# Reordering the head of a Strassen GEGLU kernel: the first product of chunk 1 and its additions earlier, the first products in halves, the last block copied whole

## The chip, the cores and the metric

The kernel runs on one core of one Trainium2 chip. Its engines are called PE (TensorE), DVE (VectorE), ACT (ScalarE), POOL (GpSimd) and SP (SyncE, which here only issues DMAs). PSUM is the memory, in banks, into which PE writes its products. The metric is the device time in microseconds (us); lower is better. Each profile is of one execution, and "the page" is the profiler's summary of it; its times count from that execution's first instruction, and "the span" is from the first to the last instruction, about 1.8 us less than the reported time.

## The reference

```python
def reference(x, w_gate, w_up, w_down):
    return (_gelu(x @ w_gate) * (x @ w_up)) @ w_down
# x: 32 x 32 x 1024 (1024 tokens of 1024), w_gate and w_up: 1024 x 3584, w_down: 3584 x 1024, all bf16
# _gelu is the tanh approximation
```

## The kernel before

Both matrix products are done by one level of the Strassen-Winograd scheme, seven products of quarter matrices instead of eight. The hidden columns of the first product go in chunks of two 128-column tiles. Chunk 0 is computed plainly, without Strassen, because its products can begin while most of x is still on its way. From chunk 1 on, TensorE (PE) multiplies sums: S1 to S4 are sums of weight quarters, T1 to T4 sums of quarters of x (b11, b12, b21, b22, transposed by the DMA but for the first part of b21). P1 is `b11` times the first quarter of the gate weights. For ten column tiles the product of `b21` with the second quarter is kept ahead: it is made in the head, copied out of PSUM to `ahead`, and added to P1 later by VectorE (DVE).

One rule of this layout matters here. P1 stays in its PSUM bank and S2*T2 is accumulated onto it. So DVE must have read P1 (the addition `c`, `c = ahead + psA`) **before** PE may start S2*T2.

The parts that the change and the argument touch (cuts marked with `...`):

```python
BANKS = {"A": 4, "B": 2, "C": 2}          # PSUM banks by tag, 128 x 512 f32 each
...
# the first quarter-tiles of b21 are transposed on PE, half by DVE, half by ACT:
for dt in range(KQ):
    for half in range(2):
        ...                                # two transposes into tp
        (nc.vector.tensor_copy, nc.scalar.copy)[half](b21[:, dt, half * hw : (half + 1) * hw], tp)
nc.tensor.matmul(warm_ps[:, : NB // 2], ...)     # a filler of 256 columns
...
for k in range(KQ):                        # the first real products
    for j in range(KB):
        product_ahead(ps[j], 0, j, k, k + 1)
...
tt(t1, b12, b11, SUB)                      # T1 on DVE
for fl in range(FC):                       # chunk 0, first 512 tokens
    ...
    plain_out(fl, 0, *tok0[fl])            # GELU on ACT, times up on DVE: "lo<-h,ps"
tok1 = [(acc("A"), acc("C")) for _ in range(FC)]
...
tt(t2, b22, t1, SUB)                       # T2
nc.scalar.copy(b22r, b22)
chunk1 = sums(1, nc.vector)
for _ in range(3):
    next(chunk1)                           # S1, S2, S4 of chunk 1 on DVE
for fl in range(FC):                       # chunk 0, second 512 tokens
    ...
    plain_out(fl, 1, *tok1[fl])
...
for j, tag in enumerate("BB"):             # the last two products kept ahead
    ps = acc(tag)
    product_ahead(ps, 2, j)
    nc.scalar.copy(ahead[2][:, j, :], ps)
...
tt(t3, b22, b12, SUB)                      # T3
begun = [first_product(FC + fl) for fl in range(FC)]   # P1, then c = ahead + P1, then GELU
next(chunk1)                               # S3
tt(t4, b21, t2, SUB)                       # T4
nc.gpsimd.tensor_copy(ident[:, :1], t4[:, 0, :1])      # POOL may start its sums only after T4
...
# in every chunk: S1*T1 in banks C, then S2*T2 onto P1 in banks A, then S4*b22 in C,
# then P1 of the next chunk, S3*T3 in A
...
# the last output block, copied in two halves by two engines from one bank:
for copy, queue, c0 in ((nc.vector.tensor_copy, nc.sync, 0), (nc.scalar.copy, nc.scalar, NB // 2)):
    o = late.tile([P, NB // 2], bf16, name="o_end", tag="o_end", bufs=2)
    copy(o, banka[m][:, c0 : c0 + NB // 2])
    queue.dma_start(out=of[r0 : r0 + P, c0 : c0 + NB // 2], in_=o)
```

Of the kernel before, what the change touches and what calls it, by code (L numbers as in the profile page):

```python
# [13 lines left out]
def kernel(  # L14
# [20 lines left out]
    nc = tc.nc  # L35
    P = nc.NUM_PARTITIONS
    fp32 = mybir.dt.float32
    f32r = mybir.dt.float32r
    bf16 = mybir.dt.bfloat16
    tt = nc.vector.tensor_tensor  # L40
    ADD, SUB, MUL = ALU.add, ALU.subtract, ALU.mult

    xf = x.flatten_outer_dims()
    of = out.flatten_outer_dims()
    N, D = xf.shape
    F = w_gate.shape[1]
    NB = 512
    assert N == 2 * NB and D == 2 * NB and F % (4 * P) == 0
    DT, FT = D // P, F // P
    KD = DT // 2  # L50
    FC = 2
# [4 lines left out]
    MT = NB // P  # L56
    NWARM = 6
    KB = 4
# [32 lines left out]
    def by_batch(tiles):  # L91
        def at(k):
            b = next(i for i, (k0, k1) in enumerate(batches) if k < k1)
            return tiles[b][:, k - batches[b][0], :]

        return at

    def g_of(ft):
        k = ft % HF
        return by_batch(g_lo if ft < HF else g_hi)(k)  # L100
# [3 lines left out]
    def acc(tag):  # L104
        return ps1.tile([P, NB], fp32, name=f"ps{tag}", tag=tag, bufs=BANKS[tag])
# [4 lines left out]
    b11 = xpool.tile([P, KD, NB], bf16, name="b11")  # L110
    b21 = xpool.tile([P, KD, NB], bf16, name="b21")
    b12 = ring.tile([P, KD, NB], bf16, name="b12", tag="ring")
    b22 = ring.tile([P, KD, NB], bf16, name="b22", tag="ring")
    t1, t2, t3, t4, b22r = (xpool.tile([P, KD, NB], f32r, name=n) for n in ("t1", "t2", "t3", "t4", "b22r"))

    def x_rows(dt, nb):
# [3 lines left out]
    ahead = [  # L120
        gpool.tile([P, n, NB], fp32, name="ahead", tag=f"hi{n}", bufs=2) for n in (KB, KB, QF - KB)
    ]
# [13 lines left out]
    def load_w_all(ci, which):  # L136

        alloc_w(ci, which)
        load_w(nc.sync, ci, which, 0, KD if which == 0 and is_ahead(ci) else DT)

    def is_ahead(ci):
        return 0 < ci and (ci + 1) * FC <= FC + NAHEAD

    def quads(ci, fl=None):
        cols = slice(None) if fl is None else slice(fl * P, (fl + 1) * P)
        wg, wu = w_tiles[ci, 0], w_tiles[ci, 1]
        a12 = wg[:, KD:, cols]
        if is_ahead(ci):
            i, j = divmod((ci - 1) * FC, KB)
            a12 = a12_ahead[i][:, :, j * P : (j + FC) * P][:, :, cols]  # L150
        return wg[:, :KD, cols], a12, wu[:, :KD, cols], wu[:, KD:, cols]
# [23 lines left out]
    ones_w = nc.const_aps.tensor(1.0, [P, P], bf16)  # L175
    ones_m = nc.const_aps.tensor(1.0, [P, NB], bf16)
# [6 lines left out]
    with tc.manual_schedule():  # L183
        for eng, p0, p1 in ((nc.sync, 0, HALF), (nc.scalar, HALF, NB_P)):
            eng.dma_start(
                out=x_nat[:, p0:p1, :],
                in_=xf[p0 * P : p1 * P, KD * P : (KD + KQ) * P].rearrange("(b p) d -> p b d", p=P),
# [34 lines left out]
        warm_ps = acc("A")  # L222
# [3 lines left out]
        for dt in range(KQ):  # L226
            for half in range(2):
                hw = HALF * P
                tag = next(tags)
# [3 lines left out]
                        tp[:, b * P : (b + 1) * P], x_nat[:, half * HALF + b, dt * P : (dt + 1) * P], ident  # L233
                    )
                (nc.vector.tensor_copy, nc.scalar.copy)[half](b21[:, dt, half * hw : (half + 1) * hw], tp)
        nc.tensor.matmul(warm_ps[:, : NB // 2], lhsT=ones_w, rhs=ones_m[:, : NB // 2], start=True, stop=True)

        def plain(ps, which, fl, nb, d0, d1, first=0, last=DT - 1):
            for dt in range(d0, d1):
                nc.tensor.matmul(  # L240
                    ps,
                    lhsT=w_tiles[0, which][:, dt, fl * P : (fl + 1) * P],
                    rhs=x_rows(dt, nb),
                    start=(dt == first),
                    stop=(dt == last),
                )

        def gelu(src, tag, bufs):
            h = ework.tile([P, NB], bf16, name=tag, tag=tag, bufs=bufs)
            nc.scalar.activation(h, src, ACT.Gelu_apprx_tanh)  # L250
            return h

        def plain_out(ft, nb, gate, up):
            tt(g_of(ft)[:, nb * NB : (nb + 1) * NB], gelu(gate, "h0", 4), up, MUL)  # L254

        def prod(ps, lhs, rhs, start):
            for k in range(KD):
                nc.tensor.matmul(  # L258
                    ps,
                    lhsT=lhs[:, k, :],  # L260
                    rhs=rhs[:, k, :],
                    start=(start and k == 0),
                    stop=(k == KD - 1),
                    skip_group_check=True,
                )

        def ahead_of(ft):
            i, j = divmod(ft - FC, KB)
            return ahead[i][:, j, :]

        def product_ahead(ps, i, j, k0=0, k1=KD):
            for k in range(k0, k1):
                nc.tensor.matmul(
                    ps,
                    lhsT=a12_ahead[i][:, k, j * P : (j + 1) * P],
                    rhs=b21[:, k, :],
                    start=(k == 0),
                    stop=(k == KD - 1),
                )


        ps = [acc(t) for t in "CCAA"]
        tok0 = [(acc("A"), acc("B")) for _ in range(FC)]

        def plain0(d0, d1):
            for which in (0, 1):
                for dt in range(d0, d1):
                    for fl in range(FC):
                        plain(tok0[fl][which], which, fl, 0, dt, dt + 1, KD, KD - 1)

        for k in range(KQ):
            for j in range(KB):
                product_ahead(ps[j], 0, j, k, k + 1)
        plain0(KD, KD + KQ)
        for j, copy in enumerate((nc.scalar.copy, nc.vector.tensor_copy) * 2):
            product_ahead(ps[j], 0, j, KQ)
# [7 lines left out]
        for j, tag in enumerate("CCAA"):  # L304
            ps = acc(tag)
            product_ahead(ps, 1, j)
            (nc.scalar.copy, nc.vector.tensor_copy)[j % 2](ahead[1][:, j, :], ps)
        tt(t1, b12, b11, SUB)
        for fl in range(FC):
            for which in (0, 1):  # L310
                plain(tok0[fl][which], which, fl, 0, 0, KD, KD, KD - 1)
            plain_out(fl, 0, *tok0[fl])
        tok1 = [(acc("A"), acc("C")) for _ in range(FC)]
        for fl in range(FC):
            for which in (0, 1):
                plain(tok1[fl][which], which, fl, 1, 0, KD)
# [5 lines left out]
        for fl in range(FC):  # L322
            for which in (0, 1):
                plain(tok1[fl][which], which, fl, 1, KD, DT)
            plain_out(fl, 1, *tok1[fl])
        load_w_all(2, 1)
        for j, tag in enumerate("BB"):
            ps = acc(tag)
            product_ahead(ps, 2, j)
            nc.scalar.copy(ahead[2][:, j, :], ps)  # L330


        def added(s, ps):
            t = ework.tile([P, NB], fp32, name="c", tag="c", bufs=3)
            tt(t, s, ps, ADD)  # L335
            return t

        def snap(ps, tag):
            t = ework.tile([P, NB], fp32, name=tag, tag=tag, bufs=2)
            nc.scalar.copy(t, ps)  # L340
            return t

        def first_product(ft):
            psa = acc("A")
            prod(psa, quads(*divmod(ft, FC))[0], b11, True)
            if ft < FC + NAHEAD:
                return psa, gelu(added(ahead_of(ft), psa), "h0", 4)
            return psa, snap(psa, "sn1")

        def last_product(st):  # L350
            ft, psa, h0 = st
            prod(psa, a22rs.pop(ft), t4, False)
            tt(g_of(ft)[:, :NB], h0, psa, MUL)  # L353

        tt(t3, b22, b12, SUB)  # L355
        begun = [first_product(FC + fl) for fl in range(FC)]
        next(chunk1)
        tt(t4, b21, t2, SUB)

        nc.gpsimd.tensor_copy(ident[:, :1], t4[:, 0, :1])  # L360
        open_fts = []
        for ci in range(1, NCH):
            fts = range(ci * FC, (ci + 1) * FC)
# [8 lines left out]
            sn5, sn2, h1, h0 = [], [], [], []  # L372
            psa, first = zip(*begun)
# [16 lines left out]
            if fts[0] < FC + NAHEAD:  # L390
                h0 = first
            else:
                for fl in range(FC):
                    psb = acc("B")
                    prod(psb, quads(ci, fl)[1], b21, True)
                    h0.append(gelu(added(first[fl], psb), "h0", 4))
            begun = [first_product(ft + FC) for ft in fts] if ci + 1 < NCH else []
            for fl, ft in enumerate(fts):
                prod(psa[fl], s3[fl], t3, False)
# [51 lines left out]
        late = ctx.enter_context(tc.tile_pool(name="late", bufs=1))  # L451
# [35 lines left out]
        banka = [acc("A") for _ in range(MT)]  # L487
# [69 lines left out]
        product(banka, by_batch(a22r), by_batch(tch), tail=QF)  # L557
        for m in range(MT):
            r0 = NB + m * P
            if m < MT - 1:  # L560
                o = late.tile([P, NB], bf16, name="o_sb", tag="o_sb", bufs=MT)
                (nc.vector.tensor_copy if m % 2 == 0 else nc.scalar.copy)(o, banka[m])
                nc.scalar.dma_start(out=of[r0 : r0 + P, :NB], in_=o)
                continue

            for copy, queue, c0 in ((nc.vector.tensor_copy, nc.sync, 0), (nc.scalar.copy, nc.scalar, NB // 2)):
                o = late.tile([P, NB // 2], bf16, name="o_end", tag="o_end", bufs=2)
                copy(o, banka[m][:, c0 : c0 + NB // 2])
                queue.dma_start(out=of[r0 : r0 + P, c0 : c0 + NB // 2], in_=o)
# [1 line left out]
_INS = ['x', 'w_gate', 'w_up', 'w_down']  # L571
_OUTS = [((32, 32, 1024), 'bfloat16')]
# [25 lines left out]
```

## Time and profile before

| kernel before | value | where it is read |
|---|---|---|
| time, first three runs | 275.81 us median (275.01 to 275.81) | the timed runs |
| span of the profiled run | 273.6 us | the page |
| PE busy | 269.1 us, 98% | the page's first part |
| PE's end | 269.98 us | the timeline |
| hole in the first Strassen chunk | about 0.4 us | matmul starts in the trace |
| PE's end to the last landing of output data | 2.51 us | the trace |

From the page of the kernel before, the span, PE's busy time and the chain of waits by engine:

```profile
span 273.6 us, 3349 instructions
...
PE 269.1 (98%) x1199; PEld 187.9 (69%) x1199; DVE 198.1 (72%) x195; ACT 111.4 (41%) x183; POOL 108.1 (40%) x55
...
PE 87%; SPq 5%; DVE 4%; DMA 2%; issue 1%; ACT 0%; DVEq 0%
```

PE is the limit, so only time in which PE stands still can be won. The chain, followed back from the end, is PE for 87% of the span, but its start runs over the DMA queue (SPq), a DMA and DVE. That is the place the change works on.

PE's timeline of before where the plain products end and chunk 1 begins (start, duration, engine, source line, operation, out<-in, size, count; groups overlap because the end of a matmul is modelled). In order: the two products kept ahead, P1, S1*T1, S2*T2, S4*b22, P1 of chunk 2.

```profile
25.30 1.89 PE L273 MATMUL psB<-b,a12b 128*128 128x512 bf16 x8
27.03 1.89 PE L258 MATMUL psA<-b,wg 128*128 128x512 bf16 x8
28.57 2.21 PE L258 MATMUL psC<-t,s 128*128 128x512 f32 x8
30.84 2.11 PE L258 MATMUL psA<-t,s 128*128 128x512 f32 x8
32.80 1.99 PE L258 MATMUL psC<-b22r,s 128*128 128x512 f32 x8
34.63 1.90 PE L258 MATMUL psA<-b,wg 128*128 128x512 bf16 x8
```

From S1*T1 to S2*T2 pass 2.28 us, where 2.02 to 2.03 is the pace elsewhere. PE's weight loads (PEld) name the cause, in brackets: the idle time just before, and what ended it.

```profile
30.84 1.68 PEld L258 LDWEIGHTS psA<-t,s 128*128 128x128 f32 x8 [0.50 <-DVE c L335]
```

DVE's timeline of before shows what stood ahead of that addition. In order: T1, two GELU products, T2, S1, S2, S4, two GELU products, T3, and then `c`.

```profile
17.45 2.29 DVE L308 TENSOR_TENSOR t<-b,b 128x2048 fp32r<-128x2048 bf16 x1 [1.62 <-DMA b<-in_x_dram]
19.66 1.28 DVE L254 TENSOR_TENSOR lo<-h,psB 128x512 bf16<-128x512 bf16 x2
20.86 2.29 DVE L317 TENSOR_TENSOR t<-b,t 128x2048 fp32r<-128x2048 bf16 x1
23.06 1.22 DVE L162 TENSOR_TENSOR s<-wu 128x1024 fp32r<-128x1024 bf16 x1
24.31 1.22 DVE L163 TENSOR_TENSOR s<-s,wg 128x1024 fp32r<-128x1024 f32 x1
25.57 1.22 DVE L164 TENSOR_TENSOR s<-a12a,s 128x1024 fp32r<-128x1024 bf16 x1
26.71 1.28 DVE L254 TENSOR_TENSOR lo<-h,psC 128x512 bf16<-128x512 bf16 x2
27.91 2.29 DVE L355 TENSOR_TENSOR t<-b,b 128x2048 fp32r<-128x2048 bf16 x1
30.11 1.28 DVE L335 TENSOR_TENSOR c<-ahead,psA 128x512 f32<-128x512 f32 x2
```

DVE works without a pause from 17.45 to the addition.

Last, the tail of before, after PE's end at 269.98 (CAST is the copy out of PSUM, DMA_DIRECT2D the issue of a store on the queue of SyncE or ACT):

```profile
270.02 0.42 DVE L568 CAST o_end<-psA 128x256 bf16<-128x256 f32 x1 [0.90 <-PE psA L421]
270.47 0.36 SPq L569 DMA_DIRECT2D out_dram<-o_end  x1
270.48 0.37 ACT L568 CAST o_end<-psA 128x256 bf16<-128x256 f32 x1 [3.04 <-DVE o_end L568]
270.88 0.34 ACTq L569 DMA_DIRECT2D out_dram<-o_end  x1
```

The two half copies run one after the other; ACT waited for DVE.

### The profile page before, as it was taken

The numbers are of one execution on the slowest core, as the hardware profiler recorded it, in microseconds if no ns is written. First come the engines' busy times: TensorE is split into PE (matmuls) and PEld (weight loads), VectorE is DVE, ScalarE is ACT, GpSimd is POOL, SyncE is SP. The second block draws the span as 40 slices with busy tenths as digits, with TensorE's granted clock in tenths as the row PEclk, the third lists the DMA queues.
The fourth block names the chain that finished last, engine by engine and source line by source line (L and its number), as shares of the span: only waits on it lengthen the run. The fifth ranks groups of instructions, "written<-read, shape, count | busy, mean of one in ns | idle before, by whom it ended". The sixth has DMA issues, their size and how long they took to land.

```text
span 273.6 us, 3349 instructions
## 1 busy us (share of the span) xinstructions
PE 269.1 (98%) x1199; PEld 187.9 (69%) x1199; DVE 198.1 (72%) x195; ACT 111.4 (41%) x183; POOL 108.1 (40%) x55
## 2 busy tenths in 40 slices
PE   8999999999999999999999999999999999999994
PEld 3444677877878677676868676764447888888883
DVE  0269997987966676666657656459999999999511
ACT  2263565454643646555463636430300023962001
POOL 1000089999897695948577574000000000000000
PEclk9999999999999999999999999999999999999999
DMA  7994330414504505050514280004992445695202
GB/s 173 282 240 127 101 90 25 117 42 114 156 16 137 146 8 157 0 153 1 154 35 120 74 274 0 0 2 163 350 293 79 134 134 189 216 285 194 78 0 78
DMA packets 53393, 33.77 MB, mean 123 GB/s; under 512 B 8704, under 2 KB 53376, under 8 KB 53376
## 3 DMA queue, kind: packets, MB, share of 16 engines
q1 hardware_dynamic: 50384, 31.13, 39.4%
q10 hardware_dynamic: 2992, 2.43, 2.7%
q8 instruction: 9, 0.15, 0.2%
q14 instruction: 8, 0.07, 0.1%
HBM read 29.62 MB, written 2.10 MB: 116 GB/s over the span
## 4 chain that ended last, share of the span: by engine, by line
PE 87%; SPq 5%; DVE 4%; DMA 2%; issue 1%; ACT 0%; DVEq 0%
PE psA L258 34%; PE psA L421 18%; PE psC L258 17%; PE psC L421 7%; PE psB L421 7%; PE psB L258 5%; SPq L205 3%; DMA b<-in_x_dram 2%; DVE lo L254 1%; SPq L134 1%; DVE t L355 1%; DVE t L317 1%; SPq L194 1%; DVE s L163 0%; DVE s L162 0%
## 5 line engine op out<-in xcount | busy, mean ns | idle before, releaser
L258 PE MATMUL psA<-t,s 128*128 128x512 f32 x208 | 54.3, 403 | 0.1
L250 ACT ACTIVATE h<-c 128x512 bf16<-128x512 f32 x52 | 31.8, 630 | 38.9 <-DVE c L335 38.9
L258 PEld LDWEIGHTS psA<-t,s 128*128 128x128 f32 x208 | 39.0, 188 | 9.7 <-DVE c L335 0.5
L162 POOL TENSOR_TENSOR s<-wu 128x1024 fp32r<-128x1024 bf16 x12 | 26.8, 2232 | 23.4 <-DMA wu<-in_w_up_dram 14.0
L335 DVE TENSOR_TENSOR c<-sn,psA 128x512 f32<-128x512 f32 x26 | 17.8, 683 | 16.8 <-PE psA L258 16.5
L258 PEld LDWEIGHTS <-wg 128*128 128x128 bf16 x168 | 15.4, 98 | 20.1 <-issue 3.4
L163 POOL TENSOR_TENSOR s<-s,wg 128x1024 fp32r<-128x1024 f32 x12 | 27.8, 2314 | 0.9
L165 POOL TENSOR_TENSOR s<-wg,wu 128x1024 fp32r<-128x1024 bf16 x12 | 27.1, 2255 | 0.0
L340 ACT COPY sn<-psC 128x512 f32<-128x512 f32 x26 | 15.2, 588 | 27.1 <-PE psC L258 23.0
L340 ACT COPY sn<-psA 128x512 f32<-128x512 f32 x42 | 23.4, 585 | 6.2 <-PE psA L258 6.1
L258 PE MATMUL psC<-t,s 128*128 128x512 f32 x104 | 25.9, 391 | 0.0
L258 PE MATMUL psA<-t,a22r 128*128 128x512 f32 x104 | 25.9, 391 | 0.0
L258 PE MATMUL psC<-b22r,s 128*128 128x512 f32 x104 | 25.7, 389 | 0.0
L258 PE MATMUL psA<-b,wg 128*128 128x512 bf16 x104 | 24.6, 380 | 0.0
L258 PEld LDWEIGHTS psC<-t,s 128*128 128x128 f32 x104 | 19.5, 188 | 4.2
L258 PEld LDWEIGHTS psA<-t,a22r 128*128 128x128 f32 x104 | 19.5, 188 | 4.1
L258 PEld LDWEIGHTS psC<-b22r,s 128*128 128x128 f32 x104 | 19.5, 188 | 4.1
L400 DVE TENSOR_TENSOR lo<-c,h 128x512 bf16<-128x512 f32 x12 | 21.5, 1794 | 0.6
L335 DVE TENSOR_TENSOR c<-sn,psC 128x512 f32<-128x512 f32 x26 | 17.7, 687 | 5.1 <-PE psC L258 5.1
L353 DVE TENSOR_TENSOR hi<-h,psA 128x512 bf16<-128x512 bf16 x14 | 9.6, 688 | 14.2 <-PE psA L258 14.2
L164 POOL TENSOR_TENSOR s<-wg,s 128x1024 fp32r<-128x1024 bf16 x8 | 17.3, 2159 | 0.6
L464 ACT COPY snb<-psC 128x512 f32<-128x512 f32 x4 | 2.2, 590 | 36.5 <-PE psC L421 22.7
(101 smaller groups left out, 411.9 us busy)
## 6 DMA issues: line engine op xcount, KB each, us to landing
wu<-in_w_up_dram SPq DMA_DIRECT2D x13, 512.0 KB, 4.0
wdb<-in_w_down_dram SPq DMA_DIRECT2D x12, 512.0 KB, 4.8
wdb<-in_w_down_dram SPq DMA_DIRECT2D x12, 384.0 KB, 4.1
wg<-in_w_gate_dram SPq DMA_DIRECT2D x8, 512.0 KB, 5.1
v<-in_w_down_dram SPq DMA_DIRECT2D x4, 512.0 KB, 6.4
out_dram<-o_sb ACTq DMA_DIRECT2D x15, 128.0 KB, 1.7
wg<-in_w_gate_dram SPq DMA_DIRECT2D x6, 256.0 KB, 4.5
v<-in_w_down_dram SPq DMA_DIRECT2D x4, 384.0 KB, 7.8
```

Of the source, the lines that this page charges most:

```text
L162: yield eng.tensor_tensor(s1, a21, a22, ADD)
L163: yield eng.tensor_tensor(s2, s1, a11, SUB)
L164: yield eng.tensor_tensor(s4, a12, s2, SUB)
L165: yield eng.tensor_tensor(s3, a11, a21, SUB)
L205: nc.sync.dma_start_transpose(out=t[:, d0 % KD : (d1 - 1) % KD + 1, :], in_=xf[nb * NB : (nb + 1) * NB, d0 * P : d1 * P])
L250: nc.scalar.activation(h, src, ACT.Gelu_apprx_tanh)
L258: nc.tensor.matmul(ps, lhsT=lhs[:, k, :], rhs=rhs[:, k, :], start=(start and k == 0), stop=(k == KD - 1), skip_group_check=True,)
L335: tt(t, s, ps, ADD)
L340: nc.scalar.copy(t, ps)
L353: tt(g_of(ft)[:, :NB], h0, psa, MUL)
L400: tt(g_of(ft)[:, NB:], added(sn5[fl], psa[fl]), h1[fl], MUL)
L421: nc.tensor.matmul(banks[m], lhsT=lhs(k)[:, m * P : (m + 1) * P], rhs=rhs(k), start=(start and k == 0), stop=(k == HF - 1), skip_group_che ...
```

## The change

The intent is to let no wait stand in front of PE at the head, and to shorten the tail. It has three pieces. Piece 1: P1 of chunk 1 goes ahead of the last two products kept ahead (which move from banks B to C, as the second tokens' up products move from C to B); its additions go ahead of T3, S3 and T4 and of the second tokens' GELU products; T1 follows the first GELU product. Piece 2: the filler goes, and the first four products are done in halves of 256 columns, so that the halves that DVE copies can be used before ACT has copied the others. Piece 3: the last block is copied whole.

```diff
-        nc.tensor.matmul(warm_ps[:, : NB // 2], lhsT=ones_w, rhs=ones_m[:, : NB // 2], start=True, stop=True)
...
         for k in range(KQ):
-            for j in range(KB):
-                product_ahead(ps[j], 0, j, k, k + 1)
+            for cols in (slice(0, NB // 2), slice(NB // 2, NB)) if k == 0 else (slice(None),):
+                for j in range(KB):
+                    product_ahead(ps[j], 0, j, k, k + 1, cols)
...
-        tt(t1, b12, b11, SUB)
         for fl in range(FC):
             for which in (0, 1):
                 plain(tok0[fl][which], which, fl, 0, 0, KD, KD, KD - 1)
-            plain_out(fl, 0, *tok0[fl])
-        tok1 = [(acc("A"), acc("C")) for _ in range(FC)]
+            plain_out(fl, 0, gelu(tok0[fl][0], "h0", 4), tok0[fl][1])
+            if fl == 0:
+                tt(t1, b12, b11, SUB)
+        tok1 = [(acc("A"), acc("B")) for _ in range(FC)]
...
-            plain_out(fl, 1, *tok1[fl])
+            tok1[fl] = gelu(tok1[fl][0], "h0", 4), tok1[fl][1]
         load_w_all(2, 1)
-        for j, tag in enumerate("BB"):
-            ps = acc(tag)
-            product_ahead(ps, 2, j)
-            nc.scalar.copy(ahead[2][:, j, :], ps)
...
+        p1 = [acc("A") for _ in range(FC)]
+        for fl in range(FC):
+            prod(p1[fl], quads(1, fl)[0], b11, True)
+        for j, tag in enumerate("CC"):
+            ps = acc(tag)
+            product_ahead(ps, 2, j)
+            nc.scalar.copy(ahead[2][:, j, :], ps)
+        begun = [first_product(FC + fl, p1[fl]) for fl in range(FC)]
         tt(t3, b22, b12, SUB)
-        begun = [first_product(FC + fl) for fl in range(FC)]
         next(chunk1)
         tt(t4, b21, t2, SUB)
 
         nc.gpsimd.tensor_copy(ident[:, :1], t4[:, 0, :1])
+        for fl in range(FC):
+            plain_out(fl, 1, *tok1[fl])
...
         for m in range(MT):
             r0 = NB + m * P
-            if m < MT - 1:
-                ...
-                continue
-            for copy, queue, c0 in ((nc.vector.tensor_copy, nc.sync, 0), (nc.scalar.copy, nc.scalar, NB // 2)):
-                ...
+            o = late.tile([P, NB], bf16, name="o_sb", tag="o_sb", bufs=MT)
+            (nc.vector.tensor_copy if m % 2 == 0 else nc.scalar.copy)(o, banka[m])
+            nc.scalar.dma_start(out=of[r0 : r0 + P, :NB], in_=o)
```

More of the change, by code (lines that the diff above doesn't have):

```diff
@@ L251, in gelu, with plain_out @@
             return h
-        def plain_out(ft, nb, gate, up):
-            tt(g_of(ft)[:, nb * NB : (nb + 1) * NB], gelu(gate, "h0", 4), up, MUL)
+        def plain_out(ft, nb, h, up):
+            tt(g_of(ft)[:, nb * NB : (nb + 1) * NB], h, up, MUL)
         def prod(ps, lhs, rhs, start):
@@ L269, in ahead_of, with product_ahead @@
             return ahead[i][:, j, :]
-        def product_ahead(ps, i, j, k0=0, k1=KD):
+        def product_ahead(ps, i, j, k0=0, k1=KD, cols=slice(None)):
             for k in range(k0, k1):
                 nc.tensor.matmul(
-                    ps,
+                    ps[:, cols],
                     lhsT=a12_ahead[i][:, k, j * P : (j + 1) * P],
-                    rhs=b21[:, k, :],
-                    start=(k == 0),
+                    rhs=b21[:, k, cols],
+                    start=(k == 0 and not cols.start),
                     stop=(k == KD - 1),
+                    skip_group_check=True,
                 )
@@ L341, in snap, with first_product @@
             return t
-        def first_product(ft):
-            psa = acc("A")
-            prod(psa, quads(*divmod(ft, FC))[0], b11, True)
+        def first_product(ft, psa=None):
+            if psa is None:
+                psa = acc("A")
+                prod(psa, quads(*divmod(ft, FC))[0], b11, True)
             if ft < FC + NAHEAD:
@@ L559 @@
             r0 = NB + m * P
-            if m < MT - 1:
-                o = late.tile([P, NB], bf16, name="o_sb", tag="o_sb", bufs=MT)
-                (nc.vector.tensor_copy if m % 2 == 0 else nc.scalar.copy)(o, banka[m])
-                nc.scalar.dma_start(out=of[r0 : r0 + P, :NB], in_=o)
-                continue
-            for copy, queue, c0 in ((nc.vector.tensor_copy, nc.sync, 0), (nc.scalar.copy, nc.scalar, NB // 2)):
-                o = late.tile([P, NB // 2], bf16, name="o_end", tag="o_end", bufs=2)
-                copy(o, banka[m][:, c0 : c0 + NB // 2])
-                queue.dma_start(out=of[r0 : r0 + P, c0 : c0 + NB // 2], in_=o)
+            o = late.tile([P, NB], bf16, name="o_sb", tag="o_sb", bufs=MT)
+            (nc.vector.tensor_copy if m % 2 == 0 else nc.scalar.copy)(o, banka[m])
+            nc.scalar.dma_start(out=of[r0 : r0 + P, :NB], in_=o)
 _INS = ['x', 'w_gate', 'w_up', 'w_down']
```

## The prediction

> **What bounds the kernel now.** TensorE: the page's first part has PE busy 269.1 of 273.6 us (98%), the chain of waits is 87% PE. Consecutive matmul starts in the trace (0.216 us apart in bf16, about 0.227 in f32) show only these holes after the warm-up: about 0.1 us before the first product (start 4.58), 0.42 us in the first Strassen chunk (28.57 to 34.63: 6.07 us where later chunks' pace gives 5.65), and 3.6 us after PE's end at 269.97.
>
> **Piece 1, P1's additions ahead (the core).** In the timeline S2*T2 starts at 30.84; its weight load waited 0.50 us for DVE's addition `c`, which stood in DVE's queue behind T1, T2, S1, S2, S4, four GELU products and T3 (2.29) and ran at 30.11. After: P1 runs on PE at about 25.2 to 27, the two last kept-ahead products follow, and DVE adds right after S4. S1 needs w_up, which lands at 22.83, S2 w_gate at 23.67, so I expect the additions at about 26.5 to 27.8, some 2.5 us before PE wants them. T3, S3, T4 end near 30, 31.2, 33.4, all before their products. The two delayed GELU products end near 34.6; DVE's next addition starts as before. POOL's sums, released by T4, start 1.5 us earlier. The hole closes: -0.40.
>
> T1 after the first GELU product costs DVE 0.1 us (b12 lands only at 17.35). The second tokens' up products now use the B banks; the second is freed near 20.5, wanted at 20.9: the tightest new wait, at most 0.3 us. The C banks of the kept-ahead products are copied by ACT about 0.1 us before S1*T1 wants them: possible +0.1.
>
> **Piece 2, first products in halves, filler matmul gone.** The matmul work is equal (eight of 256 columns for four of 512); the filler filled a wait. The first half can start at about 4.3, but the second needs the bank that ACT is copying until 4.53: at most 0.1 us won. That is then lost again: the next weights landed at 6.06 with PE loading them at 6.10, the a12 weights at 7.94 with the load at 7.98. I give it 0 to -0.05. The clock is full at 4.25 already (256 columns took 273 ns); the Trainium skill ("TensorE: Matmul & The Clock Gate", What's actually happening) has the throttle released after about 3.4 us of activity, which fits the warm-up from 0.77 to about 4.1 here.
>
> **Piece 3, last block whole.** Now DVE (0.425) and ACT (0.373) copy the halves one after the other. The Trainium skill ("PSUM — Partial Sum Buffer", PSUM bank collisions raise a hardware error) gives the reason: two engines may not read one bank at once. The last store is issued at 270.88 and lands 1.58 us later. One ACT copy of 0.59 lets a 128 KB store go at about 270.64, with 1.68 us to landing as the earlier whole blocks: about -0.15.
>
> **Sum.** -0.40 -0.15 -0.03: about -0.6 of 275.8. The three times before span 0.8 us, so the number is uncertain by as much. Predicted 275.1 us, 80% range 274.5 to 275.8; faster by over 2%: 0.01, within 2%: 0.985, slower: 0.005.
>
> **Signs.** Right: S2*T2 starts without a wait for `c`, 2.03 us after S1*T1; PE pace unbroken from 25 to 38; first full product still near 4.6 and the matmuls at 8.03 unmoved; last landing about 1.7 us after an issue 0.64 us after PE's end; no new wait at the up products at 20.9.
>
> **Wrong if.** The B or C bank waits are longer than estimated, chunk 1's weights land later, POOL's earlier start slows DVE, the DMA landings at 6 to 8 us move (then piece 2 wins 0.1 or more), or the clock's release moves.

## The result, and the profile after

| | before | after |
|---|---|---|
| time, median (range), 6 runs each | 275.81 us (275.01 to 276.0) | 275.22 us (274.86 to 275.94) |
| ratio of the mean times, 95% interval | | 0.9989 (0.997 to 1.0008) |
| span of the profiled run | 273.57 us | 273.19 us |
| P1/kept-ahead stretch to P1 of chunk 2 | 9.33 us | 9.02 us |
| PE's end | 269.98 us | 269.72 us |
| PE's end to the last landing of output | 2.51 us | 2.39 us |

A ratio is the mean time of one kernel's fast runs over that of the other's of the same rounds, so it is not quite the ratio of the medians. A second series of the changed kernel gave 0.999 (0.9976 to 1.0003). Neither interval excludes 1.

The page of the kernel after:

```profile
span 273.2 us, 3351 instructions
...
PE 268.9 (98%) x1202; PEld 188.4 (69%) x1202; DVE 193.8 (71%) x194; ACT 112.1 (41%) x183; POOL 107.1 (39%) x55
...
PE 98%; ACT 0%; issue 0%
```

The chain of waits is now PE for 98%: in this run it never leaves PE from the warm-up on. PE's timeline of after, in order P1, the two products kept ahead, S1*T1, S2*T2, S4*b22, P1 of chunk 2:

```profile
25.34 1.89 PE L257 MATMUL psA<-b,wg 128*128 128x512 bf16 x8
27.07 1.89 PE L272 MATMUL psC<-b,a12b 128*128 128x512 bf16 x8
28.77 2.11 PE L257 MATMUL psC<-t,s 128*128 128x512 f32 x8
30.72 1.99 PE L257 MATMUL psA<-t,s 128*128 128x512 f32 x8
32.54 1.97 PE L257 MATMUL psC<-b22r,s 128*128 128x512 f32 x8
34.36 1.90 PE L257 MATMUL psA<-b,wg 128*128 128x512 bf16 x8
```

S2*T2 no longer waits for `c`. But S1*T1 starts 0.16 us later after the stretch's start (28.77 - 25.34 = 3.43, before 28.57 - 25.30 = 3.27), and the second matmul of S1*T1 follows after 0.33 us instead of 0.42. Together that is about 0.07 us lost. PE's weight loads name the reason, ACT's copy out of the C bank:

```profile
28.77 1.68 PEld L257 LDWEIGHTS psC<-t,s 128*128 128x128 f32 x8 [0.31 <-ACT ahead L362]
```

DVE's timeline of after, in order: GELU product, T1, GELU product, T2, S1, S2, S4, and then `c`:

```profile
16.98 0.69 DVE L253 TENSOR_TENSOR lo<-h,psB 128x512 bf16<-128x512 bf16 x1 [1.11 <-PE psB L239]
17.59 2.28 DVE L316 TENSOR_TENSOR t<-b,b 128x2048 fp32r<-128x2048 bf16 x1
19.79 0.68 DVE L253 TENSOR_TENSOR lo<-h,psB 128x512 bf16<-128x512 bf16 x1
20.39 2.28 DVE L321 TENSOR_TENSOR t<-b,t 128x2048 fp32r<-128x2048 bf16 x1
23.45 1.23 DVE L162 TENSOR_TENSOR s<-wu 128x1024 fp32r<-128x1024 bf16 x1 [0.78 <-DMA wu<-in_w_up_dram]
24.71 1.23 DVE L163 TENSOR_TENSOR s<-s,wg 128x1024 fp32r<-128x1024 f32 x1
25.97 1.23 DVE L164 TENSOR_TENSOR s<-a12a,s 128x1024 fp32r<-128x1024 bf16 x1
27.11 1.28 DVE L335 TENSOR_TENSOR c<-ahead,psA 128x512 f32<-128x512 f32 x2
```

`c` begins at 27.11, three microseconds sooner, although S1 waited 0.78 us for its weights. The tail of after, PE's end being at 269.72:

```profile
269.75 0.58 ACT L571 CAST o_sb<-psA 128x512 bf16<-128x512 f32 x1 [2.59 <-PE psA L431]
270.37 0.34 ACTq L572 DMA_DIRECT2D out_dram<-o_sb  x1
```

The last store is issued 0.65 us after PE's end instead of 0.90.

One thing in this trace has nothing to do with the change. PE starts at half clock: its first matmuls of 512 columns start 0.43 us apart, the later ones 0.22. Before, the full clock was granted ("released") from 4.13 us on, by the trace's own record; in the profiled run of after only from 4.88 on. That cost after's head what piece 2 could have won: its products of k = 1 (the second of the 128-row steps of the first four products) start at 5.48, before's at 5.44.

### The profile page after: what moved, and what is told of

The parts are those of the page before. It is cut to its first block, busy times and chain, and to the rows that moved or that the text cites. A ratio compares the mean times of both kernels' runs of the same rounds, so it can differ in the third digit from the quotient of the medians.

```text
span 273.2 us, 3351 instructions
## 1 busy us (share of the span) xinstructions
PE 268.9 (98%) x1202; PEld 188.4 (69%) x1202; DVE 193.8 (71%) x194; ACT 112.1 (41%) x183; POOL 107.1 (39%) x55
## 4 chain that ended last, share of the span: by engine, by line
PE 98%; ACT 0%; issue 0%
PE psA L257 34%; PE psA L431 18%; PE psC L257 17%; PE psC L431 7%; PE psB L431 7%; PE psB L257 5%; PE psB L239 3%; PE psA L239 3%; PE psC L272 2%; PE psA L272 1%; PE psA L224 1%; PE tp L232 0%; ACT o_sb L571 0%
## 5 line engine op out<-in xcount | busy, mean ns | idle before, releaser
L162 POOL TENSOR_TENSOR s<-wu 128x1024 fp32r<-128x1024 bf16 x12 | 26.1, 2179 | 25.0 <-PE psC L257 16.8
L410 DVE TENSOR_TENSOR lo<-c,h 128x512 bf16<-128x512 f32 x12 | 16.9, 1405 | 0.6
L410 DVE TENSOR_TENSOR hi<-c,h 128x512 bf16<-128x512 f32 x14 | 16.9, 1205 | 0.5
```

Source lines behind the costliest of these rows:

```text
L162: yield eng.tensor_tensor(s1, a21, a22, ADD)
L410: tt(g_of(ft)[:, NB:], added(sn5[fl], psa[fl]), h1[fl], MUL)
```

## The experiments

Twelve kernels ran. The times differ by less than their spread. Two lengths serve throughout. The **stretch** runs from the end of the plain products to P1 of chunk 2. In some traces single matmul records are missing, also that of P1's first matmul; so the stretch is taken to the start of S3*T3, 1.55 us later in every complete trace, less that 1.55. The **rest** runs from S3*T3 of chunk 1 to PE's end; it was 233.81 us before and after. (The expectations count it from P1 of chunk 2, 1.55 us more: 235.36.)

### null_before: the kernel before against itself

No edit. Expected:

> The kernel before, unchanged, against itself. My theory (three small gains under a noise that comes from the moment at which TensorE's clock is released, not from the kernel): ratio 1.000 within 0.002, single times spread over 0.7 us or more, and the runs listed with a mean clock of 0.998 about 0.6 us longer than those with 1.000. In the profile the stretch from the first kept-ahead product after the plain ones (25.3) to P1 of chunk 2 (34.63) again takes 9.3 us, with S2*T2 waiting for the addition c. Rival (the difference of 0.4 to 0.6 us between the two kernels is only noise): the null run differs from its own baseline by as much, 0.4 us in the mean, and the profile's stretch varies by 0.3 us too.

Measured: 275.51 us median against 275.89, ratio 0.9984 (0.9969 to 0.9999), though both are the same program. So the times of a series of this size are uncertain by as much as the whole difference under study, and the interval, which excludes 1, was wrong here (as one in twenty should be). Listed mean clock 0.997: 275.6 and 275.78; 1.000: 275.05 to 275.79. My 0.6 us between the two did not show here.

The surprise was in the profile. The same program had **no hole**. PE's timeline of this run, S1*T1 and S2*T2:

```profile
29.04 2.18 PE L258 MATMUL psC<-t,s 128*128 128x512 f32 x8
31.05 1.98 PE L258 MATMUL psA<-t,s 128*128 128x512 f32 x8
```

The distance is 2.01 us and the stretch 8.91 us, not 9.3. The clock was granted only from 5.37 us on, so PE came to S1*T1 0.47 us later than in the first profile, and b12 had landed at 16.91 instead of 17.35, so `c` began at 29.67 instead of 30.11. My theory, that the hole belongs to the kernel, fell here, and so did the reading that the profile of before shows "the" cost. The new theory: the hole is the difference of two chains, one of DVE hanging on b12's landing, one of PE hanging on the clock's release and on weights, and either may be the later one.

### p1_alone, tail_alone, head_alone: one piece each

Edits: each kernel is the one before plus only one piece of the diff above. Expected:

> Only the first piece (P1 ahead of the last kept-ahead products, its additions ahead of T3, S3, T4, T1 after the first GELU product, the up products of the second tokens in B, their GELU products delayed); head and tail as before. My theory: the stretch of 9.33 us becomes 9.02 as in the whole change, PE's end moves from 269.98 to about 269.65 where the clock is released at the same moment, the tail from PE's end to the last landing stays at 2.48. Time -0.3 us, ratio 0.999. Rival (the piece only moves a wait to another place): the stretch shrinks but a later gap of the same size appears before PE's end, which stays near 269.98.

> Only the last block copied whole by ACT. My theory: PE's end to the last landing goes from 2.48 to about 2.36 us, everything before as in the kernel before; time -0.12 us, ratio 0.9995, not to be told from 1 by the times. Rival (a store of 128 KB takes as much longer as the copy is shorter): 2.48 or more.

> Only the halves of the first products and the filler matmul gone. My theory: with the clock released by 4.3 us (as in the profile of before) the second half-product starts at about 4.58, when ACT has read its bank, and the first products of k=1 start at about 5.35 instead of 5.44; with a later release, as in the profile of the whole change, at about 5.48. What is won there is lost or not by the weights' landing at 5.0 to 6.1. Time 0 to -0.1 us, ratio between 0.9990 and 1.0005. Rival A (removing the filler delays the clock's release): the release comes later than 4.5 us and more of its timed runs list clock 0.998 than of the null run. Rival B (the halves win 0.25, the whole wait that the filler filled): k=1 starts at 5.2.

| run | median, ratio (95%) | full clock from | k = 1 starts | stretch | tail |
|---|---|---|---|---|---|
| p1_alone | 275.28, 0.998 (0.9966 to 0.9993) | 3.77 | 5.48 | 9.01 | 2.51 |
| tail_alone | 275.09, 0.9981 (0.9963 to 0.9999) | 4.45 | 5.29 | 9.70 | 2.39 |
| head_alone | 275.68, 0.9987 (0.9972 to 1.0002) | 4.81 | 5.47 | 8.98 | 2.51 |

These ratios share the baseline of the null run (275.89), against which the same program came out 0.16% faster, so they say nothing beyond "within 0.2%".

p1_alone: the stretch is 9.01 as expected, and no gap appears later: the rest is 233.81. PE's end came to 269.77, not 269.65, because PE waited 0.06 us for weights that landed at 8.09 and started its k = 1 products 0.04 us later.

tail_alone: the tail is 2.39 us, 0.12 less than 2.51, as expected (the expectations put both tails 0.03 us shorter, at 2.48 and 2.36). The stretch was **longer** than in the kernel before, 9.70 us, though nothing was changed there. PE's weight loads of this run, for S2*T2:

```profile
31.46 1.69 PEld L258 LDWEIGHTS psA<-t,s 128*128 128x128 f32 x8 [0.84 <-DVE c L335]
```

In this run b12 landed at 17.97. This is the new theory at work, and it made a large hole in a run for which I had expected none other than before's.

head_alone: k = 1 at 5.47 with the clock released at 4.81, as expected for a late release (5.48). Its stretch, 8.98, has no hole either; b12 had landed at 16.83. Rival A, that the missing filler delays the release, got both of its signs in this run: the release came later than 4.5, and four of the six timed runs list a clock below 1.000, where the null run has two of six. All runs together give it no support: the release came between 3.42 and 5.13 us in the eight traces without the filler, and between 3.77 and 6.64 in the six with it; below 1.000 are 14 of 39 fast runs without the filler and 20 of 58 with it. (Why the listed clock is a poor sign of the release is told under "The sum" below.)

With b12's landing beside the start of `c`, the unloaded traces of kernels with before's order on both engines agree to a tenth of a microsecond (in head_alone S1 waited for w_up, which landed at 22.61, hence its 0.1 more):

| run (old order on both engines) | b12 lands | `c` begins | difference | S1*T1 + 2.02 | S2*T2 starts | stretch |
|---|---|---|---|---|---|---|
| before | 17.35 | 30.11 | 12.76 | 30.59 | 30.84 | 9.33 |
| null_before | 16.91 | 29.67 | 12.76 | 31.06 | 31.05 | 8.91 |
| tail_alone | 17.97 | 30.73 | 12.76 | 30.87 | 31.46 | 9.70 |
| head_alone | 16.83 | 29.68 | 12.85 | 30.61 | 30.63 | 8.98 |
| tail_two_banks | 17.68 | 30.44 | 12.76 | 31.52 | 31.54 | 8.95 |

`c` takes 0.68 us, so S2*T2 can start about 0.73 us after `c` begins. Where that is later than S1*T1 + 2.02, there is a hole (before, tail_alone), else there is none.

### pe_order_only, dve_order_only: which of the two reorderings makes the slack

Piece 1 moves P1 on PE and the additions on DVE. pe_order_only undoes the second, dve_order_only the first:

```diff
 # pe_order_only, against the changed kernel
+        for fl in range(FC):
+            plain_out(fl, 1, *tok1[fl])
         p1 = [acc("A") for _ in range(FC)]
 ...
-        begun = [first_product(FC + fl, p1[fl]) for fl in range(FC)]
         tt(t3, b22, b12, SUB)
+        begun = [first_product(FC + fl, p1[fl]) for fl in range(FC)]
 ...
-        for fl in range(FC):
-            plain_out(fl, 1, *tok1[fl])
 # dve_order_only, against the changed kernel
-        p1 = [acc("A") for _ in range(FC)]
-        for fl in range(FC):
-            prod(p1[fl], quads(1, fl)[0], b11, True)
         for j, tag in enumerate("CC"):
             ...
+        p1 = [acc("A") for _ in range(FC)]
+        for fl in range(FC):
+            prod(p1[fl], quads(1, fl)[0], b11, True)
```

> The whole change, but DVE's queue in the order of before: the two GELU products of the second tokens and T3 stand ahead of P1's additions; TensorE keeps the new order (P1 before the last kept-ahead products). Theory formed after the first four runs (c is ready a fixed DVE chain after a DMA has landed: in the order of before 13.5 us after b12; S2*T2 waits only where that is later than 2.0 us after S1*T1): P1 being earlier on TensorE wins nothing; c is ready 7.9 us after the later of w_up of chunk 1 landing and T2 ending, so about 30.6 to 31.9, and a hole of 0 to 1.1 us stands before S2*T2, as large as that sum says from this run's own landings. Rival (it is TensorE's order that closes the hole): S2*T2 starts 2.0 us after S1*T1 whatever the landings, and c begins by 28.5.

> The whole change, but TensorE keeps the order of before (last kept-ahead products first, then P1); DVE's queue keeps the new order. Theory: DVE's queue is what counts. c begins when P1 is done (about 28.1 and 29.0), over 1 us before it is wanted: no hole, and S1*T1 no longer waits for the C bank, so the stretch takes 8.92 us, not 9.01. But DVE idles about 1 us for P1, so T4 ends near 35.3 as before the change, POOL starts near 35.5, and S2*T2 of chunk 2 may wait up to 0.3 us (the rest after P1 of chunk 2, 235.36 in every run so far, becomes up to 235.7). Rival (TensorE's order closes the hole): S2*T2 waits for c as before.

pe_order_only: 275.23 us, ratio 0.9991 (0.9967 to 1.0015). `c` began at 29.79, not by 28.5, and ended at 30.46, 7.65 us after T2's end (22.81), where I had said 7.9. But b12 had landed very early, at 16.62, and the clock was released late (5.13), so no hole could show: stretch 9.02. The starting time of `c` speaks for DVE's queue; the hole was left undecided, which is why the last experiment was made.

dve_order_only: 275.51 us, ratio 1.0001 (0.9978 to 1.0025). `c` began at 28.26, when P1 was done; no hole, and S1*T1 did not wait for the C bank: stretch 8.95 (8.92 expected). DVE's idle moment came out behind it as expected: T4 ended at 35.35, POOL's sums started 35.66, and the weight load of S2*T2 of chunk 2 waited 0.55 us for POOL's S2. PE's timeline, S1*T1 and S2*T2 of chunk 2:

```profile
37.99 1.98 PE L257 MATMUL psC<-t,s 128*128 128x512 f32 x8
40.10 2.12 PE L257 MATMUL psA<-t,s 128*128 128x512 f32 x8
```

The rest took 234.24 us, 0.43 more than in the other runs (0.3 expected). So PE's new order is not what gives `c` its slack; it is there so that DVE has P1 in time and T4, and POOL behind it, are not late.

### before_t2_twice, after_t2_twice: a load put on both queues

If the change moved slack, a known load on DVE must cost before much and after little. T2 is computed twice (same result):

```diff
         tt(t2, b22, t1, SUB)
+        tt(t2, b22, t1, SUB)
```

> The kernel before with T2 computed twice on DVE (2.28 us more ahead of everything that follows in its queue; results unchanged). Theory: the chain from b12 to c is then 13.5 + 2.28 = 15.8 us and is exposed nearly in full: S2*T2 starts 15.8 us after b12 lands (32.7 to 33.7), the stretch takes 11.0 to 11.6 us, time +1.9 to +2.4 us, ratio 1.007 to 1.009. Rival (the hole is not DVE's queue, as the null run without a hole might suggest): no change of time beyond 0.5 us.

> The changed kernel with the same second T2. Theory: the additions had 2.4 to 3 us in hand, so the stretch stays at 9.0 to 9.1 us with no wait for c; T4 ends near 35.5, POOL starts near 35.7, and S2*T2 of chunk 2 waits 0.1 to 0.5 us for POOL. Time +0.1 to +0.5 us against the changed kernel, so about that of the kernel before: ratio 0.998 to 1.001. Rival (the change won its time elsewhere and moved no slack): +1.9 us or more, as in the kernel before.

| run | median | ratio (95%) | `c` begins | stretch | rest |
|---|---|---|---|---|---|
| before_t2_twice | 277.9 | 1.0078 (1.0049 to 1.0108) | 31.57 | 10.81 | 233.81 |
| after_t2_twice | 275.88 | 1.0013 (0.9983 to 1.0043) | 28.88 | 8.99 | 234.56 |

PE's timelines, first S2*T2 of before with T2 twice:

```profile
32.30 2.14 PE L258 MATMUL psA<-t,s 128*128 128x512 f32 x8 [1.28 <-DVE c L336]
```

and S1*T1 and S2*T2 of after with T2 twice:

```profile
28.86 2.09 PE L257 MATMUL psC<-t,s 128*128 128x512 f32 x8
30.79 1.98 PE L257 MATMUL psA<-t,s 128*128 128x512 f32 x8
```

In the kernel before 2.3 us of DVE work cost 2.2 us of time; S2*T2 started 15.8 us after b12's landing at 16.48, as expected (12.76 + 0.73 + 2.3). The stretch was a little short of the 11.0 expected because b12 came so early. In the kernel after the same work left the stretch alone. What remained (0.75 us more rest, 0.1 to 0.5 expected, so a miss) is the wait behind T4: in chunk 2 the weight loads of S1*T1 and S2*T2 waited 0.48 and 0.53 us for POOL's sums. With this load the difference between the two kernels stands clear of the noise in the times.

### both_orders, after_again: a candidate, and the changed kernel once more

Two small reorderings answer what the changed kernel still lost: ACT's bank in the first halves, and the C bank before S1*T1.

```diff
-                for j in range(KB):
+                for j in (0, 2, 3, 1) if k == 0 else range(KB):
 ...
-        for fl in range(FC):
-            prod(p1[fl], quads(1, fl)[0], b11, True)
         for j, tag in enumerate("CC"):
+            prod(p1[j], quads(1, j)[0], b11, True)
             ps = acc(tag)
```

> A candidate: the changed kernel with two small reorderings. The first half-products take the banks C, A, A, C, so that the two in A run while ACT still reads the second C bank; and P1 and the last kept-ahead products alternate, so that each C bank is copied before S1*T1 wants it. My theory: the second half-product starts 0.11 us (0.21 before the clock's release) after the first instead of 0.24, the first products of k=1 start about 0.13 us sooner than in the changed kernel for the same moment of the clock's release (5.35 instead of 5.48 for a release at 4.8), but TensorE may wait that time again for weights between 6 and 16 us; the stretch from the end of the plain products to P1 of chunk 2 takes 8.92 us instead of 9.02; rest 235.36, tail 2.39. Time -0.1 to -0.2 us against the changed kernel, too little for the times to show. Rival (the 0.1 us in the changed kernel's stretch is not the C bank): stretch 9.0.

> The changed kernel once more, on the same chip as the candidate, for its spread. My theory: stretch 9.0 us and rest 235.36 whatever the landings and the clock's release do, tail 2.39; ratio to before 0.997 to 0.9995. Rival (no real gain): ratio 1.000, as often above as below.

| run | median | ratio (95%) | full clock from | b12 lands | stretch | span |
|---|---|---|---|---|---|---|
| both_orders | 275.05 | 0.9992 (0.9978 to 1.0006) | 3.78 | 16.75 | 8.98 | 273.06 |
| after_again | 275.15 | 0.999 (0.9976 to 1.0003) | 3.92 | 17.43 | 9.02 | 272.91 |

both_orders is not faster than the changed kernel by anything the times can show. The mechanisms did work: the second half-product came 0.11 us after the first, k = 1 started at 5.25, and S1*T1 found its C bank free (its second matmul followed after the usual 0.42). The stretch fell to 8.98, not 8.92: S1*T1 of the second tile waited 0.015 us for its C bank, the other 0.05 us are spread over matmuls in steps of 0.01. And what the head won was lost within three microseconds, at weights that landed at 7.93. PE's weight loads of this run:

```profile
7.97 0.98 PEld L272 LDWEIGHTS <-a12a 128*128 128x128 bf16 x6 [0.46 <-DMA a12a<-in_w_gate_dram]
```

after_again repeats 9.02 with b12 landing at 17.43, later than in the first profile of before. (An estimate for the old DVE order: 17.43 + 12.76 + 0.73 = 30.92 for S2*T2, where S1*T1 + 2.02 was 30.53, so it would have had a hole.) Its rest is 233.81 and its tail 2.38.

### tail_two_banks: why the two half copies ran one after the other

ACT's half is read from the block before, in another bank; the result is wrong.

```diff
-                copy(o, banka[m][:, c0 : c0 + NB // 2])
+                copy(o, banka[m if c0 == 0 else m - 1][:, c0 : c0 + NB // 2])
```

> The kernel before, with ACT's half of the last block read from the block before it (another bank), so the result is wrong on purpose in 128 rows by 256 columns. My theory (the two halves ran one after the other only because they are in one PSUM bank): ACT's copy starts with DVE's or earlier, the last store is issued about 0.46 us after PE's end instead of 0.90, and PE's end to the last landing takes 2.1 us instead of 2.51, less than the 2.39 of the whole block. Rival (ACT is late for another reason, or two stores at once take longer): ACT again starts 0.46 us after DVE, or the tail takes 2.4 us or more.

The tail, PE's end being at 270.54:

```profile
270.09 0.37 ACT L568 CAST o_end<-psA 128x256 bf16<-128x256 f32 x1 [2.10 <-DMA out_dram<-o_sb]
...
270.57 0.42 DVE L568 CAST o_end<-psA 128x256 bf16<-128x256 f32 x1 [0.90 <-PE psA L421]
271.03 0.36 SPq L569 DMA_DIRECT2D out_dram<-o_end  x1
```

ACT no longer waited for DVE: with another bank the program's order between the two copies is gone, and the last store left 0.49 us after PE's end. That fits the one-bank reason. It is not a clean proof of it, because ACT's data were also ready sooner. The landing gave no verdict on the time: 15 of the store's 16 completions came by 2.10 us after PE's end, as expected, the sixteenth at 3.20. An instruction fetch of 8 KB, 0.66 us long, began 1.84 us after PE's end; that it held up that sixteenth is a guess.

### pe_order_t2_twice: the undecided question, loaded

The kernel of pe_order_only with T2 computed twice.

> The kernel of pe_order_only (TensorE in the new order, DVE's queue in the old one around P1's additions) with T2 computed twice, because b12 landed so early in the run of pe_order_only that no order would have shown a hole. My theory (DVE's queue order alone makes the slack): c is ready about 32.9 us while S2*T2 is wanted at about 30.8, so a hole of 1.7 to 2.3 us stands there, as in the kernel before with T2 twice (1.45) and unlike the changed kernel with T2 twice (none); time +1.5 to +2.2 us against before, ratio 1.005 to 1.008. Rival (TensorE's order makes the slack): no wait for c, S2*T2 starts within 2.05 us of S1*T1, and the time is within 0.5 us of before.

278.61 us, ratio 1.0081 (1.0039 to 1.0123): DVE's old order brings back the cost though PE has the new one. `c` began at 33.11 (b12 had landed late, at 18.63), and S2*T2 waited 2.44 us, somewhat over the 1.7 to 2.3 expected. So DVE's two orders, each loaded with the same second T2 under PE's new order (here and in after_t2_twice), settle it: DVE's queue makes the slack.

The run showed one more thing. Busy time of PE by stretch, with the granted clock and the DMA columns behind it: the hole, the stretch at half clock, and what followed.

```profile
31.58:33.84 2.26, 0.00 (x0) 1.00 0.00 0
34.13:37.55 3.42, 3.42 (x9) 0.50 0.00 0
37.60:45.00 7.40, 7.33 (x33) 1.00 0.30 89
```

PE stood idle for 2.26 us, and from 34.13 to 37.55, when it was busy again, its clock was halved. Two of the four timed runs, the profiled one among them, list a mean clock of 0.994 (3.41 us at half clock in 278 is that much) and took 279.5 and 279.8 us; the other two took 277.1 and 277.8. So part of the ratio 1.0081 is the clock; without it the cost is 1.3 to 1.9 us against the baseline's median of 275.82 (1.5 to 2.2 expected).

## Why the prediction was right

The measured 275.22 lies by the predicted 275.1 and inside the range. The single terms fared differently.

**The hole closes: -0.40.** The mechanism was right: DVE's queue ahead of `c`, and a fixed chain behind b12. The size was read from one profile as if it belonged to the kernel. In five unloaded traces with before's order on both engines the stretch was 9.33, 8.91, 9.70, 8.98 and 8.95, where 8.91 has no hole: a loss of 0.42, 0, 0.79, 0.07 and 0.04, with a mean of 0.26. In the profiled pair the stretch fell by 0.31.

**The C bank: possible +0.1.** It came true in every unloaded trace with the change's order on PE (after, after_again, p1_alone, pe_order_only): 9.01 or 9.02, with 0.07 to 0.08 us of wait at S1*T1. The candidate took this wait away (stretch 8.98). So where there is no hole to close, piece 1 costs up to 0.1 us (9.02 against 8.91, 8.95 and 8.98).

**The B bank, wanted at 20.9.** No wait: DVE had freed it at 20.47, the product started at 21.02.

**The additions at 26.5 to 27.8, POOL 1.5 us earlier.** Timing partly off: w_up of chunk 1 landed at 23.42 instead of 22.83, `c` ran from 27.11 to 28.39, T4 ended at 33.93 and POOL started 0.8 us earlier (34.09 for 34.89). All were still in time.

**Piece 2: 0 to -0.05.** Right. The second half-product stood at 4.58, behind ACT's copy. What an early start wins is lost at the weights' landings: both_orders won 0.13 (the second half-product 0.11 us after the first instead of 0.24) and waited at 7.97; in after_t2_twice the k = 1 products started at 4.98, 0.46 before before's, yet the plain products ended at 25.43, before's at 25.30. The Trainium skill ("TensorE: Matmul & The Clock Gate", What's actually happening) says that the window which releases the clock runs free and is not reset by the kernel. The traces agree: the release lay between 3.42 and 6.64 us over fourteen profiles, with and without the filler. Plainer still is the trace's record of the granted clock: from the release to the clock's fall behind the end of the work lay 269.65 us in twelve profiles and 266.24 in tail_two_banks, and in pe_order_t2_twice its changes lie 30.72, 3.41 and 242.35 us apart. All these are whole multiples of 3.413 us (79, 78, 9, 1 and 71), whatever the kernel did in between.

**Piece 3: -0.15.** 2.51 became 2.39 us: -0.12. All traces with the halves (2.51) and with the whole block (2.38 to 2.40) agree to 0.02 us, but for tail_two_banks. The Trainium skill ("PSUM — Partial Sum Buffer", PSUM bank collisions raise a hardware error) states that two engines reading one bank collide; the trace shows only that they are kept in order (ACT after DVE), and that the order goes with another bank.

**The sum.** That the medians of the first series differ by 0.59 us, just the predicted 0.6, is luck: the means of the same runs differ by 0.31, and the null run's median lay 0.38 below its own baseline with no change at all. An estimate from the traces is 0.28: the mean stretch is 9.17 us in the five traces of the old order and 9.01 to 9.02 in the three with piece 1 whole (after, after_again, p1_alone), which is 0.16, and the tail gives 0.12. Pooling the fast runs that list their clock, from several chips and so no more than an indication: the kernel before 275.68 us (42 runs), after 275.24 (11 runs), 0.43 apart, where I had -0.6.

The listed mean clock does not sort these runs by the moment of the release. It leaves out the half clock at the start (for 0.70 to 4.20 us of before the profile gives a clock of 1.00, though the release came at 4.13) and sinks below 1.000 where the clock falls again before the last instruction. Profiled runs that list 1.000 had their release between 3.77 and 5.37, while two that list 0.998 (before_t2_twice, after_t2_twice) had it at 4.51 and 3.46. That the change wins little when PE itself is late, because PE then hides the wait for DVE, is argued from the traces above (null_before and tail_two_banks, with the release at 5.37 and 6.64, had no hole); no run held the clock's release or b12's landing fixed.

## What to carry to other kernels

A wait of a few tenths in one profile may be the difference of two chains that both vary from run to run; compare what each hangs on (here the landing of b12 and the release of the clock) in several traces before taking its size as a gain. To find out whether a reordering moved slack that the times cannot resolve, put the same known load on the queue in both versions: 2.3 us more on DVE cost 2.2 us in the kernel before; in the changed one it left the stretch alone and made the rest 0.75 us longer. And at a packed head, an earlier start wins nothing while the next weights land when they did.

## What the Trainium skill lacked or had wrong

- "TensorE: Matmul & The Clock Gate", HAM oscillation — how this bites in real kernels: it gives as the rule that no idle gap of PE should exceed about 3.4 us. In pe_order_t2_twice a gap of 2.26 us was followed by 3.42 us at half clock (34.13 to 37.55), while PE was busy. That gap lay inside one step of the 3.41 us grid told above (30.72 to 34.13) and filled 2.26 us of it. In this one trace the gap that is safe was shorter than the page says; how much shorter is not measured (after the gap of 1.28 us in before_t2_twice the clock stayed full).
- The same page, What's actually happening: it gives the spread of the release as about 500 ns either way, though it also says that the number of slow matmuls differs from run to run. Here it lay between 3.42 and 6.64 us after the first instruction, PE being busy from 0.77 on, so up to 5.9 us after PE's start; that spread of 3.22 us is nearly a whole step of 3.41. With the release at 5.37 (null_before) and 6.64 (tail_two_banks) PE came to the end of the plain products 0.47 and 0.93 us later than with 4.13 (before), as much as this whole change or more.
- No page has, as far as I looked, how much the landing of the same DMA varies from run to run. The transposed load of b12, the same in all kernels, landed between 16.48 and 18.63 us. Most of that spread was there when the load was issued (11.24 to 13.12 us, behind the earlier loads of its queue); from issue to landing it took 5.14 to 5.88 us.
